# A fourth chunk ahead of the alternation, and two edits at the very end, in an attention and two-MoE kernel on Trainium2

## The chip, the cores and the metric

The kernel runs on one core of one Trainium2 chip. A core has a matrix engine (TensorE, PE in the rows; its weight loads are PEld), VectorE (DVE), ScalarE (ACT), GpSimd (POOL) and SyncE (SP), which issues the transfers here. The time is device microseconds of one execution. Several runs are given by their median.

## The reference

```python
def _attn_ref(q, k, v):                      # 2 x 8 heads x 768 x 64
    block, window = (32, 16)
    k_sum = k.reshape(B, H, nb, block, D).max(axis=3)
    v_sum = v.reshape(B, H, nb, block, D).mean(axis=3)
    scores_l = scale * q @ k.T               # kept where |i - j| < window
    scores_s = scale * q @ k_sum.T + np.log(block)
    a = softmax(concatenate([scores_l masked, scores_s]))
    return a @ concatenate([v, v_sum])

def _moe_ref(x, w_in, w_out, alpha):         # 1536 tokens, 512 -> 2048 -> 512
    h = x @ w_in
    g = np.maximum(h, 0.0) + alpha * np.minimum(h, 0.0)
    return g @ w_out

def _moe2_ref(x, w_in, w_out, a, b):         # the same sizes
    h = x @ w_in
    h2 = h * h
    h3 = h2 * h
    P = a[0] + a[1] * h + a[2] * h2 + a[3] * h3
    Q = 1.0 + np.abs(b[0]) * np.abs(h) + np.abs(b[1]) * h2
    g = P / (Q + 1e-06)
    return g @ w_out
```

The output is the second MoE of the first MoE of the attention.

## The kernel before

Attention is done in 24 blocks of 64 queries (12 for each batch). Its results, split into a high and a low float32r part (`xh`, `xl`), are the tokens of the MoE layers, in three tiles of 512. A layer has 16 chunks f of 128 hidden units. H of a chunk (`h_mm`) multiplies the tokens by the chunk's part of `w_in` in 12 matmuls (4 slices of 128, times high-high, low-high and high-low); its activation follows on ScalarE, VectorE and POOL, its result is split again into `gh` and `gl`, and Y of the chunk (`y_mm`) adds 12 more matmuls to the four banks `y0` to `y3`, which stay in PSUM over all chunks of a token tile. There is one `h` bank in PSUM during the attention, and one attention score bank.

Weights come as 64-bit words and are made into high and low parts on the chip, two chunks at a time: `w_split` of unit j (chunks 2j and 2j + 1) is a generator with these stages: ScalarE's `top` (L161, into the only `top` buffer), then "low": VectorE's `cv` (L163, reads `top`), which also issues the next load; then "hi": a copy on ScalarE; then "mid" and "end": one subtraction each on POOL, for the first and the second chunk. Each engine's instructions run in the order in which they are written.

The first part of the program is a loop over passes t = -1 to 27, one block of queries to a pass. In every pass the steps are taken in the order of a string in `ORDERS`: scores of block t ("qk"), Exps of block t - 1 ("exp"), pv of block t - 4 ("pv"), the key copy `kc` for block t + 1 ("k"), the steps of the weight splits, at most one H and at most one Y. In passes 10 to 13 the string begins "ks act end act gh exp qk pv hi out mid v act mask k sum gl max outl sub turn vmean Y kmax low H turned in new"; from 14 on it begins "vm act act gh act qk exp mask hi sum max pv gl inv sub out k mid v outl in turn turned vmean kmax new low guard ks Y end H". The steps "act" are the three parts of the activation of the last H: relu and multiplication by alpha on ScalarE, max on VectorE. "out" and "outl" write `xh` and `xl`, "turned" is the copy `pT`, "vm" the copy `vc<-vmean` that pv reads, "ks" the copy `kc<-kmax`.

What is done by H and Y is a list: `steps`. Tokens 0 to 255 (`first`) can begin in pass 6, tokens 256 to 511 (`second`) in pass 10; chunks 0 to 7 are done for the two halves apart, later chunks for the whole 512 tokens. A pass takes the next H if its tokens are there, its unit of `w_in` has gone through all its stages, and H is fewer than three chunks ahead of Y; it takes the next Y if its `gl` was made in an earlier pass and its unit of `w_out` is through. With N_FIRST 3 the order is first f = 0, 1, 2, then second 0, first 3, second 1, first 4, and so on.

The planner counts, for each unit, the pass at which `steps` first needs it (`need`, three more for `w_out`), and a split may begin `LEAD[j]` passes before that (`LEAD = (4, 6, 4, 4, 9, 13, 5, 10)`), one new split a pass and two under way at most, once the load is two passes old. H's of passes 6 to 13 are first 0, 1, 2, none in pass 9, second 0, first 3, second 1, first 4; the splits begin with wi2 in pass 9, wo2 in 12, wi3 in 13, wo3 in 16, wi4 in 17, then none until 20 (wi2 is unit 2 of `w_in`: chunks 4 and 5). Y's of passes 9 to 13 are first 0, first 1, first 2, none in pass 12, second 0.

After the loop a second one does the rest, one H, one Y and the activations in between to a step, without attention. In the second layer the activation is `act2_p` (absolute value, numerator and denominator), a step later `act2_q` (the division by Ln and Exp), a step later the split and Y. In a step, `act2_q` of one chunk is written ahead of `act2_p` of the next. At the end of the second layer each of the four `y` banks is copied to `stage` and sent out.

Of the kernel before, what the change touches and what calls it, by code (L numbers as in the profile page):

```python
# [17 lines left out]
ALU = mybir.AluOpType  # L18
# [10 lines left out]


START_H = 6
N_FIRST = 3
EARLY = 8

VMEAN_AT = (-1, -1, 0, 0, 1, 2, 6, 7, 8, 9, 9, 9)
# [35 lines left out]
def kernel(  # L71
# [14 lines left out]
    nc = tc.nc  # L86
# [4 lines left out]
    NC = DM // P  # L91
# [24 lines left out]
    ab = const.tile([P, 2], F32, name="ab")  # L116
# [66 lines left out]
    def x_tile():  # L183
        return tuple(xp.tile([P, NC, 512], F32R, tag=n, name=n) for n in ("xh", "xl"))
# [13 lines left out]
    def tmp(tag, n):  # L198
        return tp.tile([P, 512], F32, tag=tag, name="t" + tag, bufs=1 if tag == "v" else 2)[:, :n]
# [11 lines left out]
    def act2_p(u, f):  # L211

        n, ps = u[3], hps.pop((u, f))
        v, q, p = (tmp(tag, n) for tag in "vup")
        nc.scalar.activation(out=v, in_=ps, func=AF.Abs)  # L215
        nc.scalar.activation(out=p, in_=ps, func=AF.Identity, scale=na[:, 3:4], bias=na[:, 2:3])
        nc.gpsimd.tensor_scalar(out=q, in0=v, scalar1=ab[:, 1:2], scalar2=ab[:, 0:1], op0=ALU.mult, op1=ALU.add)  # L217
        nc.gpsimd.tensor_tensor(out=q, in0=q, in1=v, op=ALU.mult)  # L218
        nc.vector.tensor_tensor(out=p, in0=p, in1=ps, op=ALU.mult)  # L219
        nc.vector.scalar_tensor_tensor(out=p, in0=p, scalar=na[:, 1:2], in1=ps, op0=ALU.add, op1=ALU.mult)  # L220
        ts[u, f] = ps, q, p
# [22 lines left out]
    def y_mm(u, f):  # L244
        layer, i, c0, n = u
        gh, gl = gs.pop((u, f))
        wh, wl = w_chunk(layer, "wo", f)
        parts = ((wh, gh), (wh, gl), (wl, gh)) if layer == 0 else ((wh, gh), (wl, gh), (wh, gl))
        terms = [(c, m) for c in range(NC) for m in range(3)]
        if not y_list:  # L250
            terms.sort(key=lambda x: (x[0] > 1, x[0] < 2 and x[1] == 2))
        for c, m in terms:
            if f == 0 and c0 == 0 and m == 0:
                yps[c] = psy.tile([P, 512], F32, tag=f"y{c}", name=f"y{c}")
            cs = slice(c * P, (c + 1) * P)
            w, x = parts[m]
            a, b = (w[:, cs], x) if layer == 0 else (x[:, cs], w)
            nc.tensor.matmul(out=yps[c][:, c0:c0 + n] if layer == 0 else yps[c], lhsT=a, rhs=b,  # L258
                             start=(f == 0 and c0 == 0 and m == 0), stop=(f == NF - 1 and m == 2))
            if f == NF - 1 and m == 2:  # L260
                y_out(layer, i, c)

    def y_out(layer, i, c):
        ps = yps.pop(c)
        if layer == 0:
            if c == 0:
                new["x"] = x_tile()
            yh, yl = (t[:, c, :] for t in new["x"])
            nc.scalar.activation(out=yh, in_=ps, func=AF.Copy)
            nc.vector.tensor_tensor(out=yl, in0=ps, in1=yh.bitcast(F32), op=ALU.subtract)  # L270
            if c == NC - 1:
                xh[i], xl[i] = new["x"]
            return
        if c == 0:
            raw = rawp.tile([P, 2, 512], I64, tag="raw", name="stage")
            new["o"] = raw.rearrange("p a b -> p (a b)").bitcast(F32).rearrange("p (a b) -> p a b", a=NC)
        o = new["o"][:, c, :]
        if c % 2 == bool(y_list):
            nc.vector.tensor_copy(o, ps)
        else:  # L280
            nc.scalar.copy(o, ps)
        r0 = i * 512 + c * P
        nc.sync.dma_start(out=out[r0:r0 + P, :], in_=o)
# [197 lines left out]
    first, second, whole = (0, 0, 0, 256), (0, 0, 256, 256), (0, 0, 0, 512)  # L481
    n0 = N_FIRST
    steps = [(first, f) for f in range(n0)]
# [12 lines left out]
    h_list, y_list = list(steps), list(steps)  # L496
# [71 lines left out]
    with tc.manual_schedule():  # L568
# [7 lines left out]
        for t in range(-1, LAST + 1):  # L576
# [18 lines left out]
            for step in ORDERS[sum(t >= at for at in PHASES)].split():  # L595
                if step in attn:
                    f, o = attn[step]
# [34 lines left out]
    def g_all(u, f):  # L632
        g_split(u, f)
        g_low(u, f)

    order = (g_all, act2_q, act2_p, act1_all)
    with tc.manual_schedule():
        while y_list:
            now[0] += 1
            u = f = None  # L640
            if h_list and (h_list[0][0][0], "wi", h_list[0][1] // 2) in wts:
                u, f = h_list.pop(0)
                h_mm(u, f)
            w_step("low")
            for fn, u_f in sorted(late.pop(s, ()), key=lambda x: order.index(x[0])):
                fn(*u_f)
            w_step("hi")
            if u and u[0] == 0:
                late.setdefault(s + 1, []).append((act1_all, (u, f)))
                late.setdefault(s + 2, []).append((g_all, (u, f)))  # L650
            elif u:
                late.setdefault(s + 1, []).append((act2_p, (u, f)))
                late.setdefault(s + 2, []).append((act2_q, (u, f)))
                late.setdefault(s + 3, []).append((g_all, (u, f)))
            for u, f in y_list[:2]:
                if (u, f) in gs and (u[0], "wo", f // 2) in wts and (len(y_list) - len(h_list) > LAG or not h_list):
                    y_mm(*y_list.pop(0))
            w_step("mid")
            w_step("end", 2 if preps and preps[0][0] == 0 else 0 if h_list and h_list[0][0][0] == 1 and (s % 3 != 1 or h_list[0][1] < 5) else 1)
            s += 1  # L660
# [61 lines left out]
```

## Time and profile before

| | |
|---|---|
| runs | 621.86 us median of 3 (621.47 to 623.15) |
| the profiled execution | 620.94 us, its span from the first to the last instruction 618.8 us |
| TensorE busy | 594.4 us (96% of the span) |
| ScalarE, POOL, VectorE busy | 383.7, 354.8, 338.9 us |
| mean granted TensorE clock | 0.988 of full speed |

A row of a timeline gives start in us, duration in us, engine, line, operation, the tiles written and read, the size, and in brackets how long the engine was idle ahead of it and what ended that. Ends of matmuls are modelled; a group of matmuls that shows its count (x8) runs from the first to the last. Neighbours on ScalarE and VectorE overlap by about 0.1 us, so a step's cost in a row of steps is the distance of the starts.

### The profile page before, as it was taken

The numbers are of one execution on the slowest core, as the hardware profiler recorded it, in microseconds if no ns is written. First come the engines' busy times: TensorE is split into PE (matmuls) and PEld (weight loads), VectorE is DVE, ScalarE is ACT, GpSimd is POOL, SyncE is SP. The second block draws the span as 40 slices with busy tenths as digits, with TensorE's granted clock in tenths as the row PEclk, the third lists the DMA queues.
The fourth block names the chain that finished last, engine by engine and source line by source line (L and its number), as shares of the span: only waits on it lengthen the run. The fifth ranks groups of instructions, "written<-read, shape, count | busy, mean of one in ns | idle before, by whom it ended". The sixth has DMA issues, their size and how long they took to land.

```text
span 618.8 us, 8590 instructions
## 1 busy us (share of the span) xinstructions
PE 594.4 (96%) x3192; PEld 496.2 (80%) x3192; DVE 338.9 (55%) x494; ACT 383.7 (62%) x665; POOL 354.8 (57%) x343
## 2 busy tenths in 40 slices
PE   4679999999999999999999999999999999999996
PEld 2567989988888888888888888888888888888884
DVE  4766678654222111144555277776566666566664
ACT  1789798877444333367777467776566666566663
POOL 3266779675622222147777557776466666466662
PEclk9779999999999999999999999999999999999999
DMA  8898576524300000015555101000100000100001
GB/s 298 294 322 285 172 243 226 192 83 151 122 0 2 0 1 1 0 69 187 182 183 197 68 1 68 1 0 2 48 21 1 0 1 1 69 0 2 0 2 68
DMA packets 17129, 55.09 MB, mean 89 GB/s; under 512 B 2368, under 2 KB 4416, under 8 KB 12992
## 3 DMA queue, kind: packets, MB, share of 16 engines
q1 hardware_dynamic: 17088, 54.55, 26.1%
q8 instruction: 25, 0.41, 0.3%
q14 instruction: 16, 0.13, 0.1%
HBM read 51.39 MB, written 3.15 MB: 88 GB/s over the span
## 4 chain that ended last, share of the span: by engine, by line
PE 75%; DVE 10%; ACT 7%; DMA 3%; POOL 2%; issue 2%; SPq 1%; DVEq 0%; ACTq 0%
PE h L195 35%; PE y L258 35%; DVE tp L230 2%; DVE tp L220 2%; DVE h L229 2%; DVE tu L228 2%; ACT h L226 2%; ACT h L227 2%; PE s L394 1%; DVE tp L219 1%; PE po L464 1%; DMA na<-in_pa 1%; DMA raw<-in_w_in 1%; PE pt L450 1%; ACT top L161 1%
## 5 line engine op out<-in xcount | busy, mean ns | idle before, releaser
L195 PE MATMUL h<-xh,wih 128*128 128x512 f32 (+1 forms) x416 | 155.7, 374 | 0.0
L195 PE MATMUL h<-xl,wih 128*128 128x512 f32 (+1 forms) x416 | 155.2, 373 | 0.0
L195 PE MATMUL h<-xh,wil 128*128 128x512 f32 (+1 forms) x416 | 155.0, 373 | 0.0
L242 POOL TENSOR_TENSOR gl<-tp,gh 128x512 fp32r<-128x512 f32 (+1 forms) x75 | 95.2, 1269 | 80.3 <-ACT gh L137 78.9
L137 ACT ACTIVATE gh<-tp 128x512 fp32r<-128x512 f32 (+1 forms) x76 | 46.2, 608 | 91.6 <-DVE tp L230 46.0
L195 PEld LDWEIGHTS h<-xh,wih 128*128 128x128 f32 x416 | 78.3, 188 | 13.9 <-ACT kc L137 0.2
L195 PEld LDWEIGHTS h<-xl,wih 128*128 128x128 f32 x416 | 78.3, 188 | 14.0 <-issue 0.2
L195 PEld LDWEIGHTS h<-xh,wil 128*128 128x128 f32 x416 | 78.4, 188 | 13.8
L258 PE MATMUL y<-gh,woh 128*128 128x512 f32 (+1 forms) x224 | 81.9, 366 | 0.0
L258 PE MATMUL y<-gh,wol 128*128 128x512 f32 (+1 forms) x224 | 80.3, 359 | 0.0
L258 PE MATMUL y<-gl,woh 128*128 128x512 f32 (+1 forms) x224 | 80.3, 359 | 0.0
L258 PE MATMUL y<-woh,gh 128*128 128x512 f32 x192 | 74.8, 390 | 1.1 <-ACT gh L137 1.1
L163 DVE SCALAR_TENSOR_TENSOR cv<-raw,top 128x1024 int32<-128x1024 int32 x32 | 59.2, 1848 | 30.4 <-ACT top L161 23.9
L258 PE MATMUL y<-wol,gh 128*128 128x512 f32 x192 | 74.7, 389 | 0.0
L258 PE MATMUL y<-woh,gl 128*128 128x512 f32 x192 | 74.5, 389 | 0.0
L228 DVE SCALAR_TENSOR_TENSOR tu<-tu,h 128x512 f32<-128x512 f32 x48 | 33.0, 688 | 71.0 <-ACT h L227 67.5
L217 POOL TENSOR_SCALAR tu<-tv,ab 128x512 f32<-128x512 f32 x48 | 37.1, 774 | 58.0 <-ACT tv L215 58.0
L218 POOL TENSOR_TENSOR tu<-tu,tv 128x512 f32<-128x512 f32 x48 | 62.2, 1296 | 4.0
L242 POOL TENSOR_TENSOR gl<-tu,gh 128x512 fp32r<-128x512 f32 (+1 forms) x28 | 33.1, 1184 | 49.9 <-ACT gh L137 49.9
L208 DVE SCALAR_TENSOR_TENSOR tp<-h,tp 128x512 f32<-128x512 f32 (+1 forms) x28 | 17.2, 614 | 69.9 <-ACT tp L137 69.9
L226 ACT ACTIVATE h<-tu,lnb 128x512 f32<-128x512 f32 x48 | 33.2, 692 | 35.1 <-DVE tp L220 32.7
L208 DVE SCALAR_TENSOR_TENSOR tu<-h,tu 128x512 f32<-128x512 f32 (+1 forms) x28 | 17.2, 613 | 60.6 <-ACT tu L137 60.6
(79 smaller groups left out, 1061.4 us busy)
## 6 DMA issues: line engine op xcount, KB each, us to landing
raw<-in_w_in SPq DMA_DIRECT2D x16, 1024.0 KB, 4.8
raw<-in_w_out SPq DMA_DIRECT2D x16, 1024.0 KB, 4.8
qz<-in_qT SPq DMA_DIRECT2D x25, 256.0 KB, 5.3
vc<-in_vS SPq DMA_DIRECT2D x24, 192.0 KB, 5.4
kt<-in_kT SPq DMA_DIRECT2D x16, 208.0 KB, 5.4
vt<-in_vS SPq DMA_DIRECT2D x12, 256.0 KB, 5.1
out<-stage SPq DMA_DIRECT2D x12, 256.0 KB, 2.1
al<-in_alpha SPq DMA_DIRECT2D x1, 8.0 KB, 6.0
```

The source lines that it names most:

```text
L137: e.activation(out=out, in_=in_, func=AF.Copy, scale=1.0 if scale is None else scale)
L163: nc.vector.scalar_tensor_tensor(out=w.bitcast(I32), in0=rest, scalar=13, in1=top, op0=ALU.logical_shift_right, op1=ALU.bitwise_or)
L195: nc.tensor.matmul(out=ps, lhsT=a, rhs=b, start=(c == 0 and m == 0), stop=(c == NC - 1 and m == 2))
L208: nc.vector.scalar_tensor_tensor(out=t, in0=ps, scalar=0.0, in1=t, op0=ALU.max, op1=ALU.subtract)
L217: nc.gpsimd.tensor_scalar(out=q, in0=v, scalar1=ab[:, 1:2], scalar2=ab[:, 0:1], op0=ALU.mult, op1=ALU.add)
L218: nc.gpsimd.tensor_tensor(out=q, in0=q, in1=v, op=ALU.mult)
L220: nc.vector.scalar_tensor_tensor(out=p, in0=p, scalar=na[:, 1:2], in1=ps, op0=ALU.add, op1=ALU.mult)
L226: nc.scalar.activation(out=A, in_=q, func=AF.Ln, scale=2.0 ** -LN_SHIFT, bias=lnb)
L227: nc.scalar.activation(out=A, in_=A, func=AF.Exp, scale=-1.0, bias=exb)
L228: nc.vector.scalar_tensor_tensor(out=q, in0=q, scalar=one, in1=A, op0=ALU.add, op1=ALU.mult)
L242: (eng("gl") if (u, f) != steps[-1] else nc.vector).tensor_tensor(out=gl, in0=t, in1=gh.bitcast(F32), op=ALU.subtract)
L258: nc.tensor.matmul(out=yps[c][:, c0:c0 + n] if layer == 0 else yps[c], lhsT=a, rhs=b, start=(f == 0 and c0 == 0 and m == 0), stop=(f == NF ...
```

## The change

Four chunks of the first half are done ahead of the alternation in place of three. For the last chunk of all (`steps[-1]`) the two instructions that make the denominator's product, on POOL until now, go to VectorE. The copy of the last bank of the last token tile, on ScalarE until now, is made in two halves, one on VectorE and one on ScalarE.

```diff
-N_FIRST = 3
+N_FIRST = 4
...
         nc.scalar.activation(out=v, in_=ps, func=AF.Abs)
         nc.scalar.activation(out=p, in_=ps, func=AF.Identity, scale=na[:, 3:4], bias=na[:, 2:3])
-        nc.gpsimd.tensor_scalar(out=q, in0=v, scalar1=ab[:, 1:2], scalar2=ab[:, 0:1], op0=ALU.mult, op1=ALU.add)
-        nc.gpsimd.tensor_tensor(out=q, in0=q, in1=v, op=ALU.mult)
+        e = nc.gpsimd if (u, f) != steps[-1] else nc.vector
+        e.tensor_scalar(out=q, in0=v, scalar1=ab[:, 1:2], scalar2=ab[:, 0:1], op0=ALU.mult, op1=ALU.add)
+        e.tensor_tensor(out=q, in0=q, in1=v, op=ALU.mult)
...
         o = new["o"][:, c, :]
-        if c % 2 == bool(y_list):
+        if c == NC - 1 and not y_list:
+            nc.vector.tensor_copy(o[:, 0:256], ps[:, 0:256])
+            nc.scalar.copy(o[:, 256:512], ps[:, 256:512])
+        elif c % 2 == bool(y_list):
             nc.vector.tensor_copy(o, ps)
         else:
             nc.scalar.copy(o, ps)
```

## Rows read from the trace of the kernel before

**Rows 1.** The page: busy time of each engine with its share of the span, and the granted clock of TensorE in 40 equal slices, in tenths.

```profile
PE 594.4 (96%) x3192; PEld 496.2 (80%) x3192; DVE 338.9 (55%) x494; ACT 383.7 (62%) x665; POOL 354.8 (57%) x343
...
PEclk9779999999999999999999999999999999999999
```

**Rows 2.** What TensorE waited for from 60 us on: us in total, times, longest.

```profile
PE y L258 <- ACT gh L137: 1.1, 1, 1.1
PE s L394 <- ACT kc L137: 0.8, 1, 0.8
PE po L464 <- ACT vc L137: 0.7, 1, 0.7
```

**Rows 3.** Busy time of each engine in passes 10 to 15 of the attention loop, each from its first score matmul to the next pass's: length, PE, PEld, DVE, ACT, POOL, granted clock, share of the DMA engines, GB/s.

```profile
59.27:64.09 4.82, 4.82 (x51) 4.43 (x50) 3.21 (x5) 3.56 (x14) 4.18 (x5) 1.00 0.75 220
64.09:68.27 4.18, 4.18 (x38) 4.18 (x37) 2.72 (x7) 3.40 (x7) 2.72 (x4) 1.00 0.64 221
68.27:71.79 3.52, 3.52 (x42) 3.34 (x41) 2.36 (x6) 3.29 (x8) 3.35 (x5) 1.00 0.95 296
71.79:76.75 4.96, 4.96 (x55) 4.78 (x54) 3.48 (x8) 3.55 (x8) 3.32 (x5) 1.00 0.33 96
76.75:82.69 5.94, 5.12 (x55) 4.73 (x53) 2.60 (x8) 5.62 (x16) 2.58 (x4) 1.00 0.76 277
82.69:87.75 5.06, 5.06 (x52) 4.88 (x53) 5.06 (x8) 5.02 (x13) 4.63 (x5) 1.00 0.52 177
```

**Rows 4.** ScalarE in order of time: one Exp and the kmax copy of passes 11 and 12; from the top written in pass 13 to the end of pass 14's steps; the four Exps without sums of pass 15; vm of pass 18.

```profile
65.12 0.59 ACT L420 ACTIVATE p<-p 128x480 f32<-128x480 f32 x1
...
67.45 0.27 ACT L137 ACTIVATE kc<-kmax 128x96 f32<-128x96 f32 x1
...
77.04 1.38 ACT L161 ACTIVATE top<-raw 128x1024 f16<-128x1024 bf16 x1 [1.66 <-DVE cv L163]
78.29 0.35 ACT L204 ACTIVATE tu<-h 128x256 f32<-128x256 f32 x1
78.67 0.51 ACT L137 ACTIVATE tu<-tu,al 128x256 f32<-128x256 f32 x1
79.09 0.40 ACT L137 ACTIVATE gh<-tp 128x256 fp32r<-128x256 f32 x1
79.40 0.38 ACT L424 ACTIVATE p<-p,m 128x120 f32<-128x120 f32 x1
...
80.91 1.04 ACT L137 ACTIVATE woh<-cv 128x1024 fp32r<-128x1024 f32 x1
81.86 0.36 ACT L137 ACTIVATE xh<-po 128x256 fp32r<-128x256 f32 x1
82.12 0.51 ACT L137 ACTIVATE kc<-kt 128x384 f32<-128x384 f32 x1
82.54 0.58 ACT L137 ACTIVATE pT<-pt 120x512 f32<-120x512 f32 x1
83.01 0.37 ACT L204 ACTIVATE tu<-h 128x256 f32<-128x256 f32 x1
...
84.14 1.24 ACT L424 ACTIVATE p<-p,m 128x120 f32<-128x120 f32 x4
...
98.73 0.63 ACT L137 ACTIVATE vc<-vmean 24x512 f32<-24x512 f32 x1
```

**Rows 5.** From the timelines of VectorE and POOL in pass 10: the `cv` of wi2, and one subtraction of the softmax.

```profile
62.99 1.54 DVE L163 SCALAR_TENSOR_TENSOR cv<-raw,top 128x1024 int32<-128x1024 int32 x1
...
62.47 0.98 POOL L415 TENSOR_TENSOR p<-p,m 128x480 f32<-128x480 f32 x1
```

**Rows 6.** The chain of the last chunk, from its denominator on POOL to its Ln on ScalarE: timelines of VectorE, POOL and ScalarE.

```profile
604.71 0.75 DVE L230 SCALAR_TENSOR_TENSOR tp<-tp,na,h 128x512 f32<-128x512 f32 x1
605.38 0.68 DVE L219 TENSOR_TENSOR tp<-tp,h 128x512 f32<-128x512 f32 x1
606.09 0.75 DVE L220 SCALAR_TENSOR_TENSOR tp<-tp,na,h 128x512 f32<-128x512 f32 x1
...
604.63 1.29 POOL L218 TENSOR_TENSOR tu<-tu,tv 128x512 f32<-128x512 f32 x1
...
606.93 0.69 ACT L226 ACTIVATE h<-tu,lnb 128x512 f32<-128x512 f32 x1 [0.75 <-DVE tp L220]
```

**Rows 7.** Prices: groups of instructions by line and shape; busy us in all, then mean ns of one.

```profile
L139 DVE COPY kc<-kt 128x384 f32<-128x384 f32 x4 | 1.4, 351 | 0.0
L242 DVE TENSOR_TENSOR gl<-tp,gh 128x512 fp32r<-128x512 f32 x1 | 0.7, 692 | 0.8 <-ACT gh L137 0.8
...
L208 DVE SCALAR_TENSOR_TENSOR tu<-h,tu 128x256 f32<-128x256 f32 x8 | 3.3, 417 | 6.3 <-ACT tu L137 6.3
...
L204 ACT ACTIVATE tp<-h 128x256 f32<-128x256 f32 x8 | 3.1, 382 | 3.5 <-PE h L195 3.5
```

**Rows 8.** The copies of the last two banks: timelines of VectorE and ScalarE.

```profile
613.81 0.69 DVE L279 COPY stage<-y 128x512 f32<-128x512 f32 x1 [0.23 <-PE y L258]
...
614.50 0.59 ACT L281 COPY stage<-y 128x512 f32<-128x512 f32 x1 [0.80 <-PE y L258]
```

**Rows 9.** Two stretches early in the span, columns as in rows 3.

```profile
10.20:23.90 13.70, 10.14 (x66) 6.52 (x64) 9.09 (x22) 7.70 (x31) 1.05 (x3) 1.00 0.90 297
23.90:37.50 13.60, 9.88 (x64) 8.55 (x64) 8.39 (x14) 10.90 (x25) 5.63 (x5) 0.50 1.04 330
```

## Prediction

> **What bounds the kernel now.** The page comes first: TensorE is busy 96% of the span and its clock is granted at nearly full speed almost throughout [rows 1]. Then the list of what TensorE waited for after the first 60 us: three waits, 0.8, 0.7 and 1.1 us [rows 2]. So from there to the end the kernel is a queue of matmuls with 2.6 us of holes in it. An edit that only moves matmuls in this stretch can win back at most the holes near it; it can lose as much as it opens. The third view is a table by pass of the attention loop [rows 3]. I call F3 the chunk f = 3 of tokens 0 to 255 and S3 that of tokens 256 to 511, and wi2 or wo2 the third pair of weight chunks (f = 4 and 5). In the passes shown TensorE has no idle time but for the 0.82 us in pass 14, and ScalarE is close behind it: 5.62 of 5.94 us in that pass and 5.02 of 5.06 in the next. There the wait is for `kc`, the key copy that ScalarE makes for the next pass [rows 2], and what is ahead of it on ScalarE is seen in its rows in order of time [rows 4]: the `top` of a weight split, which itself waited 1.66 us for VectorE's `cv` of the split before (there is one `top` buffer), then relu, al, gh, four Exps, hi, out, and only then the key copy. Any pass into which more of this is put holds TensorE up at the next scores.
>
> **The change, part 1: N_FIRST 4.** Nothing moves before pass 9. There F3 now follows Y of F0, in a pass that had no H; it left pass 11. One H or one Y is worth 1.44 us of TensorE (a pass with both lasts 4.96, one without Y 3.52) [rows 3]. TensorE's total is unchanged and pass 9 had no hole to fill, so F3 gains nothing there: pass 10 starts at 60.7 instead of 59.27.
>
> Behind it the planner's due passes move. F4 and F5, and F6 and F7, are due two passes sooner (F4 at 11 instead of 13), so the splits do too: wo2's `top` moves from pass 12 to 10, wi3's from 13 to 12, wo3's from 16 to 14, wi4's from 17 to 15. But wi2 stays where it is (top 9, cv 10, hi 11, its last part 12), since it could not start sooner, so F4 cannot go in pass 11: that pass has no H at all, and pass 14 has no Y. From pass 20 on both orders are the same. So ScalarE gets 2.2 us more per split (top 1.25, hi 0.95 [rows 4]) in just the passes where TensorE has less. I add up ScalarE's starts from the distances in [rows 4]: relu 0.38, al 0.42, gh 0.31, Exps with sums 1.51, four Exps without 1.14, one Exp 0.5, hi 0.95, out 0.26, key copy 0.42, turned 0.47, top 1.25, kmax copy 0.27, vm 0.63.
>
> Pass 10, from 60.7: relu of F3 waits for its H, 60.9; relu, al, gh, Exps and out end at 63.8. VectorE's `cv` of wi2 stands behind the residual of that out and started 3.7 us into this pass before [rows 5]; now about 4.0, so 64.7, and it takes 1.54, until 66.3. ScalarE's top of wo2, new in this pass, must wait for it and ends at 67.6; every ScalarE step of pass 11 is queued behind it. Pass 11: kmax copy, relu, al, gh, one Exp, hi of wi2, key copy are 3.25 us, 70.9. TensorE has finished pass 11 at 60.7 + 4.82 + 4.18 - 1.44 = 68.3, so its scores of pass 12 wait some 2.7 us. Passes 12 and 13: TensorE needs 4.96 us each, and the key copies come 0.3 us ahead of it (in pass 12 the Exp waits for POOL's subtraction, 0.98 [rows 5], which is queued behind a weight part; I put that at 73.6). Pass 14, from 81.0 and without Y, takes TensorE 3.5 us; ScalarE needs from relu at 81.2 to the key copy 4.25 (with Exps with sums and hi of wi3), 85.45: a wait of 1.0. Then turned and top of wo3 until 87.2. Pass 15: 85.5 + 4.96 = 90.5 against 87.2 + relu, al, gh, four Exps, hi of wo3, out, key copy (3.88) = 91.1: a wait of 0.7. Then turned and top of wi4 until 92.8, and vm of pass 16 until 93.45, for which the pv matmuls, there at 92.2, wait 1.25. In pass 17 there is no split and ScalarE is ahead again. The new waits are 2.7 + 1.0 + 0.7 + 1.25, some 5.7 us; the old two (0.8 and 0.7) stood at steps that are re-ordered and go with them, 1.5. Net +4.2 us. The bounds: -1.5, if no new wait forms and the old ones go; +7, if besides all of these H of F4 waits in pass 12 for more of wi2's low part than its own half (one POOL part, 1.3 us).
>
> **Part 2: the last denominator on VectorE.** The end of the kernel is the last chunk's chain. POOL finished its second instruction at 604.63 + 1.29 = 605.92, but ScalarE's Ln waited until 606.93, for VectorE's L220 [rows 6], since it writes over `h`, which L220 reads. So POOL was 1 us early and VectorE was late: its queue is in order, and q of chunk 14 (L228 to L230) stands ahead. The two moved instructions now go between L230 and L219. The product costs what VectorE's subtraction of the same shape costs, 0.69; the TENSOR_SCALAR has no row of this shape: below, the copy of 128x384 from SBUF, 0.35; above, 0.69 again [rows 7]. I take 0.45, as one source from SBUF is nearest to the copy. Independent neighbours start 0.08 before the last one ends (L230 to L219: 0.67 of 0.75), dependent ones 0.03 after [rows 6]. That is 0.48 + 0.61 = 1.1 us later (1.0 to 1.35) for L219, L220, Ln and everything to the end, since TensorE already waits 1.1 us there for the last gh [rows 2]; no cover is left. A gain is excluded, as POOL did not release Ln.
>
> **Part 3: the last bank in two halves.** Before, ScalarE copied the whole bank from 614.50 in 0.59, and VectorE came free at the same moment, 613.81 + 0.69 [rows 8]. Halves of 256 columns cost about 0.42 on VectorE and 0.38 on ScalarE [rows 7]. Side by side they end 0.17 sooner; in turns, 0.42 + 0.03 + 0.38 = 0.83, 0.24 later. The trace has no two readers of one bank at the same time, so I take in turns. The Trainium skill (PSUM — Partial Sum Buffer, section "PSUM bank collisions raise a hardware error") speaks against the split: two engines that access one bank in the same partitions at once collide, reads with reads too, whatever the columns, so programs must order them. By it the halves go in turns, +0.24; by the rows of each half alone, -0.17. No row of before can show which.
>
> **Sum.** The profiled execution took 620.94 us, 0.92 under the median of the runs, 621.86. 4.2 + 1.1 + 0.25 = 5.55 gives 626.5 in its terms, 627.4 against the median. A change of 0.3%, 1.87 us, is about what can be told from none: over 623.7 is slower.
>
> **Rivals.** (a) The delays are absorbed: `cv` and `top` come sooner than I put them, the key copies of passes 11, 14 and 15 arrive in time, and what waits remain are as long as the old ones. For it: ScalarE's total is the same, and in passes 10 and 11 it was idle 1.3 and 0.8 us [rows 3]. Against it: pass 14 already lost 0.82 in just this way. Only the tail counts: 621.86 + 1.1 and between -0.17 and +0.24, so 622.8 to 623.2. (b) Not slower: with three splits pulled forward ScalarE has room exactly where TensorE waited (passes 14 and 18), both waits go and none forms, -1.5; with the tail and side-by-side halves 621.86 - 1.5 + 1.1 - 0.17 = 621.3. It decides if the key copy of pass 11 ends before 68.3; I have it at 70.9. (c) The clock. After a stretch in which TensorE was busy 10.14 of 13.7 us it was granted 0.50, the 1.2 GHz level, for the next 13.6 us [rows 9]. The new holes come in passes 12 to 16; if they drew such a stretch, half of it is lost, 6.8 us, so 634. Against it: with 5.7 us of holes in the 28 us from 68 to 97 us TensorE would still be busy 80% of the time, against 74% in that row. The Trainium skill (TensorE: Matmul & The Clock Gate, "What's actually happening") ties the clock to how busy TensorE has been recently; the row of 0.50 agrees with that. (d) The lateness piles up, since VectorE and POOL, which I held at their old pace, are late as well: part 1 at its upper bound or beyond, 630 to 632.
>
> **How the numbers follow.** The forecast (623.8 to 629.8) 0.69; (a) 0.14; (b) 0.05; (c) 0.05; (d) 0.07. Slower is the forecast, (c), (d) and a corner of (a): 0.82; within 0.3% most of (a) and (b): 0.16; faster 0.02, as even (b) stays short of 1.87. The range goes from (a), 622.8, to the upper bound of part 1 with the slower tail, 621.86 + 7 + 1.6 = 630.5.
>
> **What will show it.** In the changed kernel's waits of TensorE: one of 2 to 3 us for a ScalarE key copy near 68 to 71 us, smaller ones for `kc` and for vm near 85, 91 and 92 us, and at the end a wait for gh of about 2.2 instead of 1.1 us with Ln near 1.1 us later after its Abs. ScalarE's `top` would show a wait for `cv` near 64 to 66 us. The two half copies should follow one another. Wrong would be: key copies in time (then (a)), or an Ln no later than before, which would mean that I read the order of VectorE's queue wrongly.

## The result: 1.1% slower

| | before | after |
|---|---|---|
| runs of the comparison | 621.66 us median of 4 (621.33 to 623.15) | 628.78 us median of 4 (627.31 to 630.39) |
| ratio | | 1.011, 95% interval 1.008 to 1.014 |
| profiled execution, its span | 620.94, 618.8 | 629.28, 627.3 |
| mean granted TensorE clock | 0.988 | 0.980 |
| TensorE busy | 594.4 | 599.6 |

The forecast was 627.4 within 622.8 to 630.5, slower. It held; the sum came out 1.4 us short. Three executions (one of e4, two of the kernel before beside e9 and e10) took 1.6 to 5.4 times as long as the others and are left out of the medians below.

One thing has to be taken out before the two traces are compared. Both kernels are the same up to pass 9, but TensorE's early stretch at the 1.2 GHz level lasted from 23.9 to 37.5 in the profile of before [rows 9] and from 25.2 to 42.3 in that of after, and pass 9 began 1.13 us later (54.06 instead of 52.93). In the profiles of this study it was between some 10 us (e9) and 20 us (e5) long, and all these kernels are alike up to there. So profiles are compared here **from pass 9's first scores to the end of the span**: 565.9 us before, 573.3 after, **+7.4**. From pass 9 to pass 19 the loop went from 50.46 to 55.58 (+5.1); the rest, +2.26, is at the very end: from pass 19 to the last chunk's Abs it is 499.68 us before and 499.67 after.

The page of after, with the clock's last slice now below full speed, and what TensorE waited for from 60 us on:

```profile
PE 599.6 (96%) x3192; PEld 499.1 (80%) x3192; DVE 339.7 (54%) x497; ACT 383.1 (61%) x665; POOL 351.6 (56%) x341
...
PEclk9869899999999999999999999999999999999998
```

```profile
PE s L398 <- ACT kc L137: 3.1, 3, 1.8
PE y L259 <- ACT gh L137: 2.0, 1, 2.0
PE po L468 <- ACT vc L137: 1.2, 1, 1.2
```

2.6 us of waits [rows 2] have become 6.4. By pass (columns as in rows 3; passes 10 to 12, then 14 to 16):

```profile
61.81:66.95 5.14, 5.07 (x51) 4.50 (x49) 3.54 (x6) 3.40 (x13) 2.81 (x3) 1.00 0.44 116
66.95:71.62 4.67, 2.90 (x26) 2.70 (x24) 2.38 (x7) 4.49 (x9) 1.56 (x3) 1.00 0.72 252
71.62:78.18 6.56, 6.55 (x52) 6.33 (x53) 4.33 (x7) 3.94 (x9) 6.39 (x7) 0.74 0.66 235
...
83.14:87.76 4.62, 3.67 (x42) 3.29 (x41) 3.40 (x7) 4.39 (x15) 2.61 (x5) 1.00 0.54 177
87.76:93.35 5.59, 5.23 (x52) 4.84 (x53) 3.79 (x8) 5.56 (x13) 3.84 (x5) 1.00 0.77 248
93.35:99.72 6.37, 5.13 (x52) 4.88 (x53) 4.59 (x8) 6.28 (x12) 5.94 (x6) 1.00 0.84 291
```

In pass 11 TensorE has 2.90 us of work and ScalarE 4.49; in passes 14 and 15 ScalarE is the fuller engine again. The chain behind the longest wait, in ScalarE's, VectorE's and TensorE's rows:

```profile
65.85 1.22 DVE L163 SCALAR_TENSOR_TENSOR cv<-raw,top 128x1024 int32<-128x1024 int32 x1
...
67.10 1.38 ACT L161 ACTIVATE top<-raw 128x1024 f16<-128x1024 bf16 x1 [1.67 <-DVE cv L163]
71.06 0.51 ACT L137 ACTIVATE kc<-kt 128x384 f32<-128x384 f32 x1
...
71.62 1.15 PE L398 MATMUL s<-kc,qz 128*128 128x120 f32 x8 [1.77 <-ACT kc L137]
87.76 1.15 PE L398 MATMUL s<-kc,qz 128*128 128x120 f32 x8 [0.95 <-ACT kc L137]
93.35 1.15 PE L398 MATMUL s<-kc,qz 128*128 128x120 f32 x8 [0.36 <-ACT kc L137]
95.74 0.69 PE L468 MATMUL po<-pT,vc 120*64 120x64 f32 x16 [1.24 <-ACT vc L137]
```

The `top` of the moved split waits for `cv`, everything of pass 11 on ScalarE is behind it, and the key copy ends 71.57, when TensorE has been idle for 1.77.

The end: the last chunk's Abs, before and after, its chain on VectorE and its Ln (answers to rows 6), the last matmuls, and the two half copies (answers to rows 8).

```profile
603.07 0.59 ACT L215 ACTIVATE tv<-h 128x512 f32<-128x512 f32 x1
...
609.31 0.59 ACT L215 ACTIVATE tv<-h 128x512 f32<-128x512 f32 x1
...
610.95 0.75 DVE L231 SCALAR_TENSOR_TENSOR tp<-tp,na,h 128x512 f32<-128x512 f32 x1
611.62 0.54 DVE L218 TENSOR_SCALAR tu<-tv,ab 128x512 f32<-128x512 f32 x1
612.19 0.69 DVE L219 TENSOR_TENSOR tu<-tu,tv 128x512 f32<-128x512 f32 x1
...
613.52 0.75 DVE L221 SCALAR_TENSOR_TENSOR tp<-tp,na,h 128x512 f32<-128x512 f32 x1
...
614.30 0.69 ACT L227 ACTIVATE h<-tu,lnb 128x512 f32<-128x512 f32 x1 [1.87 <-DVE tp L221]
```

```profile
618.70 0.50 PE L259 MATMUL y<-woh,gh 128*128 128x512 f32 x1 [2.04 <-ACT gh L137]
...
622.91 0.40 PE L259 MATMUL y<-woh,gl 128*128 128x512 f32 x1
...
623.34 0.42 DVE L280 COPY stage<-y 128x256 f32<-128x256 f32 x1
623.80 0.37 ACT L281 COPY stage<-y 128x256 f32<-128x256 f32 x1 [1.91 <-DVE stage L280]
```

Ln starts 4.99 after its Abs (609.31), 3.86 before (603.07 to 606.93): +1.13. TensorE waits 0.94 longer, and its last 12 matmuls begin 9.39 after the Abs (618.70) where they began 8.33 after it (611.40): +1.06. They start over 4.21 us (618.70 to 622.91); in the trace of before it was 2.67 (611.40 to 614.07). The reason is in the clock (columns as in rows 3; the second window is in pass 12, after the wait of 1.77):

```profile
619.10:622.60 3.50, 3.50 (x10) 2.72 (x9) 0.98 (x3) 0.59 (x1) 0.00 (x0) 0.51 0.05 18
...
73.00:76.40 3.40, 3.40 (x28) 3.28 (x25) 1.83 (x5) 1.25 (x2) 3.23 (x4) 0.50 0.51 152
```

Twice, shortly after a wait of about 2 us, the engine ran at the 1.2 GHz level for some 3.4 us. At the end that is 4.21 - 2.67 = 1.54 us. The last copy ends 0.24 later behind the last matmul, and the span ends 0.59 sooner behind that copy, so the end is 1.06 + 1.54 + 0.24 - 0.59 = 2.25 of the 2.26. The last two belong together. Behind the copies the four banks' transfers have to go out, and in the trace of before they fill the DMA engines without a gap from 614.4 to 617.1, and likewise in e4, the halves alone (columns as in rows 3; before, then e4):

```profile
614.40:617.10 2.70, 0.06 (x1) 0.00 (x0) 0.10 (x1) 0.59 (x1) 0.00 (x0) 1.00 1.00 376
617.55:620.30 2.75, 0.05 (x1) 0.00 (x0) 0.52 (x2) 0.37 (x1) 0.00 (x0) 1.00 1.00 374
```

From the last copy to the end it is 3.74 us before, 3.50 in e4, where that copy ends 0.24 later, and 3.15 in after. So what the copies, or slower matmuls, lose is in part taken back by the transfers: the half clock and the halves together cost 1.2 at the end and not 1.8.

### The profile page after: what moved, and what is told of

Same layout as the page of the kernel before. It is cut to its first block, busy times and chain, and to the rows that moved or that the text cites. A ratio compares the mean times of both kernels' runs of the same rounds, so it can differ in the third digit from the quotient of the medians.

```text
span 627.3 us, 8584 instructions
## 1 busy us (share of the span) xinstructions
PE 599.6 (96%) x3192; PEld 499.1 (80%) x3192; DVE 339.7 (54%) x497; ACT 383.1 (61%) x665; POOL 351.6 (56%) x341
## 3 DMA queue, kind: packets, MB, share of 16 engines
HBM read 51.39 MB, written 3.15 MB: 87 GB/s over the span
## 4 chain that ended last, share of the span: by engine, by line
PE 76%; DVE 9%; ACT 7%; DMA 4%; issue 1%; POOL 1%; SPq 1%; DVEq 0%; ACTq 0%
PE h L195 35%; PE y L259 35%; PE s L398 2%; DVE tp L231 2%; DVE tp L221 2%; DVE h L230 2%; DVE tu L229 2%; PE po L468 2%; PE pt L454 2%; ACT h L227 2%; ACT h L228 1%; DMA kt<-in_kT 1%; DVE tp L220 1%; DMA na<-in_pa 1%; PE vps L363 1%
## 5 line engine op out<-in xcount | busy, mean ns | idle before, releaser
L219 POOL TENSOR_TENSOR tu<-tu,tv 128x512 f32<-128x512 f32 x47 | 60.9, 1296 | 3.9
```

Of the source, the lines that this page charges most:

```text
L219: e.tensor_tensor(out=q, in0=q, in1=v, op=ALU.mult)
```

## The experiments

Edits are to the kernel before. "From pass 9" is the profiled execution from pass 9's first scores to the end of its span, against 565.9 before.

| kernel | median, us | before beside it | ratio (95%) | from pass 9 |
|---|---|---|---|---|
| e1 four ahead alone | 627.34 | 622.58 | 1.0079 (1.0066 to 1.0092) | +4.5 |
| e2 four ahead, old splits | 625.15 | 622.58 | 1.0042 (1.0028 to 1.0055) | +2.3 |
| e3 denominator on VectorE | 624.54 | 622.58 | 1.0030 (1.0018 to 1.0042) | +1.0 |
| e4 last bank in halves | 623.04 | 622.58 | 1.0005 (0.9993 to 1.0018) | 0.0 |
| e5 four ahead, splits spread | 623.47 | 622.64 | 1.0014 (1.0000 to 1.0028) | +0.8 |
| e6 three ahead, splits spread | 620.87 | 622.64 | 0.9971 (0.9956 to 0.9986) | -1.9 |
| e7 last quotient in SBUF | 622.17 | 622.64 | 0.9996 (0.9984 to 1.0008) | -0.7 |
| e8 = e6 + e7 | 620.03 | 622.64 | 0.9961 (0.9946 to 0.9977) | -2.6 |
| e9 = e3 again | 624.52 | 622.18 | 1.0025 (1.0006 to 1.0044) | +1.7 |
| e10 = e3, the wait filled | 623.92 | 622.18 | 1.0021 (1.0005 to 1.0037) | +1.0 |

### The three parts, each alone

```diff
 # e1
-N_FIRST = 3
+N_FIRST = 4
 # e3
+        e = nc.gpsimd if (u, f) != steps[-1] else nc.vector
+        e.tensor_scalar(...)
+        e.tensor_tensor(...)
 ...
 # e4
+        if c == NC - 1 and not y_list:
+            nc.vector.tensor_copy(o[:, 0:256], ps[:, 0:256])
+            nc.scalar.copy(o[:, 256:512], ps[:, 256:512])
 ...
```

> The kernel before with N_FIRST 4 alone. If the three parts add up, as I worked them out and as the changed kernel's trace shows them (pass 19 begins 5.1 us later beyond what was lost before pass 9, the tail costs 1.1 for the denominator, about 1.5 for a stretch of half clock at the end and 0.24 for the halves), this one is 3.5 to 5.5 us slower than before: 625 to 627, with TensorE waits for the key copy of ScalarE near passes 12, 15 and 16 and for vm in pass 16, some 4.3 us together, and the wait for the last gh back at 1.1. Rival: the loss is mostly in the tail; then this kernel is within 2 us of before.

> The kernel before with the last denominator on VectorE alone. Theory: Ln of the last chunk comes 1.1 us later after its Abs (5.0 instead of 3.9), TensorE's wait for the last gh is 2.0 to 2.2 us, and the time is 1.1 us longer, 622.7; 2.5 us longer, 624.2, in executions in which that wait also draws a stretch at half clock over the last 12 matmuls. Rival, POOL was the late one: Ln no later, the time the same or 0.5 shorter.

> The kernel before with the last bank's copy in two halves alone. In turns: VectorE's half about 0.42, then ScalarE's 0.37, the end 0.24 us later than with one copy of 0.59, which the times cannot tell from before (621.9 by the sum). Side by side: 0.17 sooner.

The medians move by 4.8, 2.0 and 0.5 (the last within its interval of none), 7.2 together; the whole change moved 7.1. So the medians add up, and part 1 is two thirds. The waits of e1 are those of after, but for the end's:

```profile
PE s L394 <- ACT kc L137: 3.1, 4, 1.8
PE po L464 <- ACT vc L137: 1.2, 1, 1.2
PE y L258 <- ACT gh L137: 1.1, 1, 1.1
```

The loop from pass 9 to pass 19, in before, in e1, and in e6 (below), which does before's matmuls and waits for nothing (columns as in rows 3):

```profile
52.93:103.39 50.46, 48.94 (x485) 45.16 (x484) 37.57 (x71) 45.62 (x108) 40.49 (x43) 1.00 0.66 214
...
54.78:109.78 55.00, 50.45 (x484) 45.52 (x483) 37.22 (x72) 46.01 (x108) 43.32 (x46) 1.00 0.63 208
...
55.24:103.84 48.60, 48.60 (x484) 45.09 (x483) 34.93 (x71) 43.81 (x106) 39.67 (x44) 1.00 0.67 215
```

Of e1's 4.5 us, TensorE's idle time is 3.0 (4.55 for 1.52) and its busy time 1.5 (50.45 for 48.94), without any half-clock stretch there. So the same matmuls took longer. Pass 10 is 0.31 longer, at H of S0, whose tokens' low part is just being written (here in after: VectorE until 65.47, the matmul that reads it 65.53):

```profile
65.05 0.42 DVE L482 TENSOR_TENSOR xl<-po,xh 128x256 fp32r<-128x256 f32 x1 [0.41 <-ACT xh L137]
...
65.53 0.38 PE L195 MATMUL h<-xl,wih 128*128 128x256 f32 x1
```

In pass 12 of e1 another 0.3: POOL, busy 5.65 of 5.82 us, makes `gl` behind a weight part, and Y's second matmul starts as it ends (0.50 after the first; it is 0.20 elsewhere).

```profile
71.97 1.27 POOL L173 TENSOR_TENSOR wil<-cv,wih 128x512 fp32r<-128x512 f32 x1 [2.65 <-ACT wih L137]
73.20 1.71 POOL L242 TENSOR_TENSOR gl<-tp,gh 128x256 fp32r<-128x256 f32 x1
...
74.47 0.36 PE L258 MATMUL y<-gh,woh 128*128 128x256 f32 x1
74.97 0.39 PE L258 MATMUL y<-gl,woh 128*128 128x256 f32 x1
```

And each wait costs more than the list of waits says. The eight score matmuls after one last 1.15 where others last 1.04, and TensorE is busy some 5.12 us in a pass beside a wait that it does in 4.96 elsewhere; [rows 3] have it too, in pass 14 with its 5.12. Without before's two waits, 1.52 us, the loop of e6 is 1.86 shorter. What is left of e1's busy time, about 0.9, stands beside its five waits; e6 shows such a cost for before's two, for e1's it is the likely reading.

In e3's profile gh is awaited 2.0 us, Ln starts 4.99 after its Abs, as in after, and the clock does not fall: +1.0. In e4 the halves go in turns, and the last copy ends 1.25 after the last matmul starts, where it was 1.02; the end of the span is no later (0.0), for the transfers' sake:

```profile
617.64 0.42 DVE L279 COPY stage<-y 128x256 f32<-128x256 f32 x1
618.10 0.37 ACT L280 COPY stage<-y 128x256 f32<-128x256 f32 x1 [1.23 <-DVE stage L279]
```

### Is it where the splits go, or the order of H and Y itself?

```diff
 # e2
-N_FIRST = 3
+N_FIRST = 4
-LEAD = (4, 6, 4, 4, 9, 13, 5, 10)
+LEAD = (4, 6, 2, 2, 5, 13, 5, 10)
 # e5: N_FIRST = 4 and
+LEAD = (4, 6, 3, 2, 4, 13, 5, 10)
```

> N_FIRST 4, and LEAD = (4, 6, 2, 2, 5, 13, 5, 10), so that the weight splits of units 2 to 4 begin in the passes of before (wo2 12, wi3 13, wo3 16, wi4 17) while H and Y keep the order that N_FIRST 4 gives them (no H in pass 11, no Y in pass 14). Theory 1, the earlier splits crowd ScalarE in passes with little TensorE work: the wait ahead of pass 12 is gone (no top of wo2 stands ahead of pass 11's steps), those of passes 15 and 16 shrink, waits after 60 us are 1 to 2.5 us in all, and the time is 621.5 to 623.5. Theory 2, the order of H and Y alone does it (a pass without H is too short for ScalarE's steps, whatever splits are in it): the waits stay near 4 us and the time near e1's.

> N_FIRST 4 with LEAD = (4, 6, 3, 2, 4, 13, 5, 10): wo2's top in pass 11 and its hi in 13, wi3 as in e2 (top 13, hi 15), wo3 16, wi4 18. So pass 14, the one without Y, has no split step on ScalarE, and no pass has two. e2 kept 0.4 us of waiting at pass 11, which has no H, 0.5 for the single h bank and 1.3 for the key copy of pass 14, which had the hi of wo2. If these 1.3 are ScalarE's crowding (theory 1), they shrink to 0.3 or less here, the wait for vm (0.8 in e2) goes too, and from pass 9 to the end this kernel is within 1 us of before (e2 was 2.4 us longer): 622.0 to 623.7. If the pass without Y is too short whatever stands in it (theory 2), 1 us or more stays ahead of pass 15 and the time is like e2's, 625.

My theory had 621.5 to 623.5 for e2, with 1 to 2.5 us of waits; 625.15 is a miss, halfway, and the waits, 4.1 in all, are those of theory 2. The wait ahead of pass 12 shrank from 1.78 to 0.44 as the theory says, but with the splits where they were, others are left:

```profile
PE s L394 <- ACT kc L137: 1.7, 2, 1.3
PE y L258 <- ACT gh L137: 1.1, 1, 1.1
PE po L464 <- ACT vc L137: 0.8, 1, 0.8
PE h L195 <- DVE tp L208: 0.5, 1, 0.5
```

The last row is new: in pass 14, which has no Y now, TensorE comes to its H before VectorE has read the one `h` bank. As its splits run in the passes of before, e2's 2.6 us (625.15 against 622.58) come with the new order alone, and the earlier splits of e1 add 2.2. So the order of H and Y has a cost of its own, about half of part 1: a pass without H and one without Y are short for TensorE, and ScalarE's and VectorE's steps in them are not. e5, with the splits spread, brings the waits of the loop down to 0.8 for `kc` and 0.6 for that bank, less in sum than before, and stands at 623.47, 0.14% over before with an interval that starts at none. So better places take back nearly all of part 1's loss. They don't make the order free: e6 below has the old order with its splits spread, and is 2.6 us under e5 (620.87 for 623.47, their intervals apart). Pass 14 of e5, without Y, shows it (columns as in rows 3):

```profile
82.61:87.62 5.01, 4.05 (x41) 3.42 (x40) 2.33 (x7) 4.98 (x16) 3.80 (x5) 1.00 0.76 250
```

TensorE needed 3.52 for such a pass [rows 3, pass 12]; ScalarE is busy for 4.98 of the 5.01 and has no room in it. Among its work is still the `top` of a split (82.94 to 84.31) that is written in pass 13, so what the order costs at the best places, no run shows.

### If places are what matters, three ahead can gain from them

```diff
 # e6
-LEAD = (4, 6, 4, 4, 9, 13, 5, 10)
+LEAD = (4, 6, 5, 4, 4, 13, 5, 10)
 # e7, in act2_p
-        ts[u, f] = ps, q, p
+        ts[u, f] = ps if (u, f) != steps[-1] else v, q, p
 # e8: both
```

> The kernel before (N_FIRST 3) with LEAD = (4, 6, 5, 4, 4, 13, 5, 10): wo2's top moves from pass 12 to 11 (hi from 14 to 13) and wi4's from 17 to 19; H and Y as before. If ScalarE's crowding is what TensorE waits for after 60 us, the 0.8 us ahead of pass 15 and the 0.7 for vm in pass 18 both go and nothing takes their place: 1.5 us less than before from pass 9 to the end, 620.4 to 621.3. If the waits belong to the passes and not to the splits, they stay, and the time is that of before.

> The kernel before, POOL keeps the last denominator, and for the last chunk alone the Ln and what follows write the SBUF tile v in place of the h bank, so that Ln need not wait until VectorE's L220 has read h. If VectorE was the late one at the end, as I read it, Ln of the last chunk begins when POOL has finished, 1.0 us sooner after its Abs (2.9 instead of 3.9), TensorE's last wait for gh falls from 1.1 to 0.2 us, and the end comes 0.9 us sooner: 621.0 to 621.7. Rival: POOL was the late one, or the three VectorE steps behind Exp queue behind L220 all the same; then nothing is gained.

> e6 and e7 together on the kernel before: if both hold, 1.5 and 0.9, some 2.4 us less than before, 619.5 to 620.5, with no wait of TensorE over 0.5 us after 60 us.

In e6 the two waits of the loop are gone and gh alone is left, 1.1 as before: 0.29% faster (0.14 to 0.44). e7 takes the other way to shorten the last chain: Ln writes over `v` in SBUF and not over `h`, so it need not wait for VectorE's L220, which still reads `h`. Ln starts 607.49, 3.02 after its Abs where before it was 3.86, and the wait for gh is 0.3 (I had put 2.9 and 0.2). What it comes behind now is ScalarE's own `gh` of the chunk before (606.95 to 607.58):

```profile
607.49 0.71 ACT L226 ACTIVATE tv<-tu,lnb 128x512 f32<-128x512 f32 x1
...
PE y L258 <- ACT gh L137: 0.3, 1, 0.3
```

Its 0.7 us are in the profile; the runs, 622.17 against 622.64, cannot tell them from nothing. e8 has both, its only wait after 60 us is those 0.3, and at 620.03 it beats both kernels: 0.39% (0.23 to 0.54) under before. It also tests how I read the chain's end: POOL's product was early, and what held Ln was a VectorE instruction for the sake of a buffer. Moving POOL's work to VectorE lengthened just that.

A second `top` buffer would have tested the wait for `cv` by itself; it was not tried, so that this wait makes the first of the new ones rests on the rows alone.

### Why the runs of e3 lost more than its chain

e3's runs stand 2.0 us above before, its profile only 1.0 from pass 9, and the profile of after has the half clock in its last matmuls. So either the longer wait draws that stretch in some executions, or the median is made otherwise. e9 is e3 again; e10 fills the wait with eight matmuls whose result nothing uses.

```diff
 # e10, in y_mm, last chunk of all, after the order of the matmuls
+            fill = psh[count[0] % len(psh)].tile([P, 512], F32, tag="h", name="h")
+            for _ in range(8):
+                nc.tensor.matmul(out=fill, lhsT=wl[:, 0:P], rhs=wh, start=True, stop=True)
```

> The same kernel as e3, as the comparison for e10 on one chip. If the two groups of times in e3 (about 623.0 and 625.2, with mean clocks near 0.985 and 0.981) come from a stretch at half clock that the 2.0 us wait for the last gh draws in some executions, they are seen again: part of the runs 0.4 to 1.1 us over before, part 2.3 to 2.8 over it.

> e3's kernel with eight more matmuls of 128x512 into a free bank between Y of chunk 14 and Y of the last chunk (their result is not used), some 1.8 us of work in the 2.0 us wait. If the wait draws the half clock, the upper group of times is gone and all runs lie 0.4 to 1.3 us over before; the matmuls cost nothing, as they end before gh does. If the clock falls for another reason, both groups stay.

The end of e9, its wait and its clock (columns as in rows 3):

```profile
PE y L259 <- ACT gh L137: 2.0, 1, 2.0
...
613.90:617.30 3.40, 2.78 (x7) 1.67 (x5) 1.36 (x2) 1.17 (x2) 0.00 (x0) 0.50 0.50 187
```

and of e10:

```profile
611.65 1.98 PE L255 MATMUL h<-woh,wol 128*128 128x512 f32 x8
...
PE y L262 <- ACT gh L137: 0.2, 1, 0.2
...
613.80:617.00 3.20, 3.06 (x12) 2.17 (x12) 2.08 (x3) 0.64 (x2) 0.00 (x0) 1.00 0.03 13
```

e9 is the same program as e3, and this time the clock fell behind the 2.0 us: the last 12 matmuls start over 3.64 us, and from pass 9 it is +1.7 where e3 was +1.0. With the wait filled they take 2.67, and the kernel is +1.0 from pass 9, the chain alone. So at the profiles' level: a half-clock stretch came behind the longer wait in after and e9 but not in e3, and with the wait filled the chain is left; as e3 was without it too, one profile of e10 does not show that filling prevents it. At the level of the runs it is not settled. e10 was to lose the upper group of e3's times (624.1 to 625.6); its runs are 620.92 to 624.96 with half above 623.9, and its median is 1.74 over before, not 1.0. What the other 0.7 are stays open; the early stretch, which differs from execution to execution, makes runs differ by as much.

## Why the prediction was right, and where it was off

- **The mechanism of part 1** held at each step. `cv` of wi2 started 4.04 into pass 10 (4.0), `top` of wo2 waited for it, pass 11's steps on ScalarE took 3.23 (3.25), and the four new waits stand where they were put, for `kc`, `kc`, `kc` and `vc`, with the old two gone. The forecast did not price the order and the earlier splits apart; by e2 the order alone is about half.
- **The first wait was mis-sized**: 1.77, not 2.7. `cv` took 1.22 and not the 1.54 of its one row, so the key copy came 0.45 sooner; and TensorE was 0.45 later, as it lost 0.3 in pass 10 and took 2.90, not 2.74, in pass 11. The others: 0.95 (1.0), 0.36 (0.7), 1.24 (1.25). In sum 4.3 for 5.7.
- **What was left out** made up for it: 0.3 in pass 10 for `xl`, 0.3 in pass 12 for `gl`, made behind a weight part on POOL (I had kept a late POOL for the upper bound only, and for H), and about 0.9 around the waits, since I priced a wait at its idle time alone. So part 1 is +4.5 in e1, for +4.2: nearly right by two errors that cancel, which is luck.
- **Part 2**: +1.13 from Abs to Ln, forecast 1.1. TENSOR_SCALAR took 0.54 and not 0.45, within its bounds. That cover was gone, and that a gain was excluded, is right.
- **Part 3**: the copy ended 0.24 later, as forecast, but the step from there to the end was wrong: the sum put the copy on the path, and the transfers behind it took the 0.24 back (e4: 0.0 from pass 9). The two halves go in turns. That agrees with the Trainium skill (PSUM — Partial Sum Buffer, section "PSUM bank collisions raise a hardware error"), by which accesses to one bank by two engines have to be kept apart: ScalarE's half starts 0.04 after VectorE's has ended, in after and in e4.
- **The missing 1.4 us** is rival (c) in small, by the one profile of after: from pass 9 it is 1.8 over the sum (7.4 for 5.55), and the half clock is worth about that. I gave it 6.8 us in a stretch of 13.6 like the early one, and looked for it only in passes 12 to 16. It came in stretches of some 3.4 us, once there, where later waits and the late `gl` would have cost most of it anyway (+5.1 against +4.5 in e1: 0.6), and once at the end, where, of its 1.5 and the halves' 0.24, 1.2 reached the end of the span. Whether each of the four runs has both, the record does not show. The argument against (c), an average of 80% busy over 28 us, was the wrong one: the two stretches followed single waits.
- Rivals (a) and (b) fell with the key copy of pass 11, which ended 71.57; pass 9 began 1.13 later than in the trace the forecast was worked out on, so that is 70.4 there, 2.1 after the 68.3 that would decide. (d) did not come: the waits did not grow from pass to pass.

## What to carry to other kernels

In a loop whose matrix engine is nearly full, a reordering that keeps every engine's total can still cost: draw up each in-order engine's work by pass, and put moved work where the matrix engine is long, not where the plan's due times fall (two numbers of `LEAD` are worth 1.7 us between e2 and e5, and 1.8 between before and e6). A pass that keeps the other engines' steps but loses half of TensorE's has a price too: with the splits spread in both, the new order is 2.6 us behind the old one (e5, e6). Before work goes from one engine to another to shorten a chain, look at which engine released the chain's next step, and for what; here it was a buffer reused too early (e7), and the engine that got the work was the one that was late. Price a wait in a dense stretch at more than its idle time (1.86 us for 1.52 between before and e6). At the very end, look at whether the last copy or the transfers behind it end the span.

## What of the hardware was not expected

- **Half-clock stretches of some 3.4 us in dense work.** After waits of 1.77 and 2.04 us in after and of 2.02 in e9 the granted clock was 0.50 or 0.51 for about that long; after the same waits in e1 (1.78) and e3 (2.0) it stayed at 1.00. From pass 8 to the last matmul no profile shows one after waits of 1.5 and less, and every one has some. The Trainium skill (TensorE: Matmul & The Clock Gate, section "What's actually happening") ties the clock to how busy the engine has been of late and says that where it changes varies from run to run of one kernel; the same waits with and without the stretch agree with the second, and that each stretch came right behind a wait does not speak against the first. Why one execution draws it and the next does not, no run here shows.
- **The early stretch varies by execution.** The kernels are alike before pass 9, and still the clock came back at 37.5 in the profile of before [rows 9], at some 37 in e9, at some 45 in e8 and 47 in e5, and in after at 42.3 (columns as in rows 3):

```profile
25.20:42.30 17.10, 11.99 (x80) 9.11 (x78) 11.50 (x20) 13.06 (x30) 9.87 (x9) 0.50 1.04 345
```

- TENSOR_SCALAR with two pointer scalars on 128x512 takes 0.54 on VectorE, between the copy of 128x384 (0.35) and the subtraction of the same shape (0.69) [rows 7].
